# Loading w2 in one transfer of 14 rows per partition instead of one of 12 rows and eight small ones

## Chip, cores, metric

One core of a Trainium2 chip. The metric is the device time of one execution in microseconds (us); lower is better.

## The reference, cut to what matters

```python
# x: (2, 1, 512) bf16; K, V caches: (2, 32, 8192, 128) bf16; w1: (512, 1792); w2: (1792, 512)
xn  = layernorm(x)
out = x + attention(xn, k_cache, v_cache, wq) @ wo + relu(xn @ w1) @ w2
```

One decode step. The caches are 268 MB of the 280 MB that are read; w2 is 1.8 MB.

## The kernel before

The SP engine issues every large load on one queue, in the order in which the data are wanted. The dense branch (`w1`, `w2`) is computed ahead of the loop over 32 cache blocks ("steps").

```python
FA = FT - 2            # 12 rows of w2 on every partition
FB = 2 * (FT - FA)     # 4 more on 64 partitions
FJ = FA + FB
...
# SP
sp.dma_start(vs[1], wq)                                                  # 4 MB
sp.dma_start(w1_sb, B_w1...).then_inc(dW1, 16)                           # 1.8 MB
sp.dma_start(w2_sb[:, 0:FA, :], B_w2[0:P * FA, :]...).then_inc(dW2, 16)  # 1.5 MB
w2_v = B_w2[P * FA:, :].rearrange("(p j) n -> p j n", j=FB)
for p in (0, 1, 2, 3, 32, 33, 34, 35):                                   # 8 x 32 KB
    sl = slice(p, p + 29, 4)
    sp.dma_start(w2_sb[sl, FA:FA + FB, :], w2_v[sl]).then_inc(dW2b, 16)
load_k(0); load_k(1); load_v(0)                                          # 4 MB each
for t in range(NP - 2):
    sp.wait_ge(pT[NG - 1], t + 1)   # PE has transposed K of step t: its buffer is free
    load_k(t + R)
    sp.wait_ge(sW, t + 1)
    load_v(t + 1)
...                                  # last V in two halves, then wo in five pieces, then the output
# PE, ahead of the loop
for j in range(FJ):                  # h^T = (xn @ w1)^T, four matmuls for each j
    ...
for j in range(FJ):                  # y = relu(h) @ w2
    half = slice(0, HP if j >= FA else P)
    pe.matmul(y, lhsT=hT[half, j, :], rhs=w2_sb[half, j, :], ...)
```

Of the kernel before, what the change touches and what calls it, by code (L numbers as in the profile page):

```python
# [7 lines left out]
ALU = mybir.AluOpType  # L8
# [11 lines left out]
def kernel(  # L20
# [13 lines left out]
    P = 128  # L34
    HP = P // 2
# [8 lines left out]
    FT = Dff // P  # L44
# [9 lines left out]
    QH = 512 // Dh  # L54
    Z = (QG - 1) * Bsz

    FA = FT - 2
    FB = 2 * (FT - FA)
    FJ = FA + FB
    inv_sqrt = float(Dh) ** -0.5  # L60
    eps = 1e-5

# [8 lines left out]
    def sem(name):  # L71
        return tc.alloc_semaphore(name)
# [6 lines left out]
    w1_sb = w_sb[:, 0:KT * Dff].rearrange("p (kt f) -> p kt f", kt=KT)  # L79
    w2_sb = w_sb[:, KT * Dff:KT * Dff + FJ * D].rearrange("p (j n) -> p j n", j=FJ)  # L80
# [30 lines left out]
    hT = sb([P, FJ, Bsz], bf16, "hT")  # L111
# [16 lines left out]


    dX, dO, dW1 = sem("dX"), sem("dO"), sem("dW1")  # L130
    dW2, dW2b = sem("dW2"), sem("dW2b")
    dK = [sem(f"dK{i}") for i in range(R)]
    dV = [sem(f"dV{i}") for i in range(R)]
    dH = [sem(f"dH{i}") for i in range(2)]
# [7 lines left out]
    sH, sF, sZ = sem("sH"), sem("sF"), sem("sZ")  # L142
# [13 lines left out]
    )  # L156
    hp = ot[1][:, 0:FJ * Bsz].rearrange("p (j b) -> p j b", b=Bsz)
    y = Sc[1][0:Bsz, :]
# [13 lines left out]
    @(lambda f: f(nc.sync))  # L172
    def _(sp):
        sp.dma_start(w1_sb, B_w1.rearrange("(p kt) f -> p kt f", kt=KT)).then_inc(dW1, 16)
        sp.dma_start(
            w2_sb[:, 0:FA, :], B_w2[0:P * FA, :].rearrange("(p j) n -> p j n", j=FA)
        ).then_inc(dW2, 16)

        w2_v = B_w2[P * FA:, :].rearrange("(p j) n -> p j n", j=FB)
        for p in (0, 1, 2, 3, 32, 33, 34, 35):  # L180
            sl = slice(p, p + 29, 4)
            sp.dma_start(w2_sb[sl, FA:FA + FB, :], w2_v[sl]).then_inc(dW2b, 16)
        load_k(0)
        load_k(1)
        load_v(0)
        for t in range(NP - 2):
            sp.wait_ge(pT[NG - 1], t + 1)
# [3 lines that stand above are left out]
        sp.wait_ge(sW, NP - 1)  # L191
        for i in range(2):
            sl = slice(i * SLOT // 2, (i + 1) * SLOT // 2)
            sp.dma_start(  # L194
                vs[(NP - 1) % R][:, sl], V_all[(NP - 1) * P:NP * P, sl]
            ).then_inc(dH[i], 16)
        for c in range(NC):
            sl = slice(cuts[c], cuts[c + 1])
            sp.dma_start(wo_sb[:, sl, :], wo_v[:, sl, :]).then_inc(dW[c], 16)  # L199
        sp.wait_ge(sE, 1)  # L200
        sp.dma_start(
            out.rearrange("b s (c p) -> (b s c) p", p=P), osb[:]
        ).then_inc(dO, 16)
# [38 lines left out]
    def _(pe):  # L242
# [7 lines left out]
        for g in range(QG):  # L250
            for kt in range(KT):
                i = pe.matmul(  # L252
                    qp,
                    lhsT=xz[:, kt, Z - g * Bsz:Z - g * Bsz + QG * Bsz],
                    rhs=vs[1][:, (kt * QG + g) * 512:(kt * QG + g + 1) * 512],
# [3 lines left out]
        i.then_inc(sQ, 1)  # L259
        pe.wait_ge(dW1, 16)  # L260

        w1_a = w1_sb[:, :, 0:P * FA].rearrange("p kt (f j) -> p kt j f", j=FA)
        w1_b = w1_sb[:, :, P * FA:].rearrange("p kt (f j) -> p kt j f", j=FB)
        for j in range(FJ):
            for kt in range(KT):
                i = pe.matmul(  # L266
                    hp[0:HP if j >= FA else P, j, :],
                    lhsT=w1_b[:, kt, j - FA, :] if j >= FA else w1_a[:, kt, j, :],
                    rhs=xz[:, kt, Z:Z + Bsz],
                    start=(kt == 0),  # L270
                    stop=(kt == KT - 1),
                )
# [6 lines left out]
        i.then_inc(sQ, 1)  # L279
        pe.wait_ge(sF, 2)  # L280
        pe.wait_ge(dW2, 16)
        pe.wait_ge(dW2b, 16 * 8)
        for j in range(FJ):
            half = slice(0, HP if j >= FA else P)
            i = pe.matmul(  # L285
                y,
                lhsT=hT[half, j, :],
                rhs=w2_sb[half, j, :],
                start=(j == 0),
                stop=(j == FJ - 1),  # L290
            )
# [82 lines left out]
        for u in range(2):  # L374
            t = pe.matmul(dbp[:, :, u], lhsT=onesh[:, u, :], rhs=RS[:], start=True, stop=True)
        t.then_inc(sH, 1)
        for k in range(KT):
            pe.matmul(
                fin[:, k, :],
                lhsT=ys[:, k * P:(k + 1) * P],  # L380
                rhs=ident2[:],
# [10 lines left out]
        for b in range(Bsz):  # L392
            t = pe.transpose(tO[:, b, :], OTn[:, b, :], identb[:])
# [3 lines left out]
        for dq in range(DQ):  # L397
            t = pe.matmul(
                ox,
                lhsT=sel[:, dq, :],  # L400
                rhs=Ob[:, :, dq * WJ:(dq + 1) * WJ],
                start=(dq == 0),
                stop=(dq == DQ - 1),
            )
# [3 lines left out]
        for c in range(NC):  # L408
            pe.wait_ge(dW[c], 16)
            for j in range(cuts[c], cuts[c + 1]):  # L410
                for k in range(KT):
                    t = pe.matmul(
                        fin[:, k, :],
                        lhsT=wo_sb[:, j, k * P:(k + 1) * P],
                        rhs=OX[:, j, :],
# [14 lines left out]
    @(lambda f: f(nc.vector))  # L430
    def _(v):
        v.memset(eps_t[:], eps).then_inc(sV, 1)
        v.memset(onesb[:], 1.0)
        v.memset(xz[:], 0.0).then_inc(sZ, 1)
        v.memset(prm[R - 1][:], 0.0).then_inc(sP, 1)
        v.wait_ge(dX, 16)
        v.bn_stats(out=stats[:], in_=xsb[:]).then_inc(sV, 1)
        v.wait_ge(sV, 2)
        v.bn_aggr(out=mv[:], in_=stats[:]).then_inc(sV, 1)
        v.wait_ge(sA, 1)  # L440
        v.reciprocal(out=rinv[:], in_=rstd[:]).then_inc(sV, 1)
        v.wait_ge(sV, 4)

        v.tensor_scalar(
            out=xn[:],
            in0=xsb[:].rearrange("b (p kt) -> b kt p", kt=KT),
            scalar1=mv[:, 0:1],
            scalar2=rinv[:, 0:1],
            op0=ALU.subtract,
            op1=ALU.mult,  # L450
        ).then_inc(sV, 1)
        v.wait_ge(sQ, 1)
        v.wait_ge(sZ, 1)
        v.tensor_copy(xz[:, :, Z:Z + Bsz], tpx).then_inc(sV, 1)
        v.wait_ge(sQ, 2)

        v.tensor_scalar(  # L457
            out=qs[:], in0=qp, scalar1=inv_sqrt, scalar2=None, op0=ALU.mult
        ).then_inc(sV, 1)
        v.wait_ge(sF, 1)  # L460
        for sl in (slice(0, P), slice(0, FA)), (slice(0, HP), slice(FA, FJ)):
            t = v.tensor_scalar(
                out=hT[sl], in0=hp[sl], scalar1=0.0, scalar2=None, op0=ALU.max,
            )
        t.then_inc(sF, 1)
        v.wait_ge(sQ, 3)

        v.tensor_copy(
            qb[:].rearrange("p (b g l) -> p l g b", b=Bsz, l=QH),
            tpq.rearrange("p l (g b) -> p l g b", b=Bsz),  # L470
        ).then_inc(sV, 93)
        v.wait_ge(sF, 3)
        v.tensor_tensor(out=ys[:], in0=y, in1=xsb[:], op=ALU.add).then_inc(sF, 1)

        def pair(i, n):
            for e in range(NG):
                if e not in ON_ACT:
                    v.wait_ge(pT[e], n)
                    kcopy(v, e)
            v.wait_ge(sS, n)  # L480
            for u in range(2):
                half = slice(u * HP, (u + 1) * HP)
                m = v.tensor_reduce(  # L483
                    out=mcol[i][half, :], in_=S_of(i)[half, :, u], axis=AX.X, op=ALU.max
                )
            m.then_inc(sM, 1)
            v.wait_ge(sT, n)
            v.tensor_reduce(  # L488
                out=mx[i][:], in_=tr_of(i).rearrange("o (u m) -> o u m", u=2),
                axis=AX.X, op=ALU.max, negate=True,  # L490
            ).then_inc(sX, 1)

        reg = nc.alloc_register(mybir.EngineType.DVE, "pairno_v")
        v.reg_mov(reg, 0)
        with v.Fori(0, NP // R):
            for r in range(R):
                v.reg_add(reg, reg, 1)
                pair(r, reg)

        v.wait_ge(sH, 1)  # L500
        v.reciprocal(out=RD[:], in_=Sc[0][:, 0:N]).then_inc(sV, 1)
        v.wait_ge(sV, 101)
        v.wait_ge(sO, NP + 1)
        on = OTn[:].rearrange("p b h -> p (b h)")
        v.tensor_tensor(
            out=on[:, 0:N - 2], in0=OTf[:, 2:N], in1=RD[:, 0:N - 2], op=ALU.mult
        ).then_inc(sV, 1)
        v.wait_ge(sW, NP + 1)
        v.tensor_tensor(
            out=on[:, N - 2:N], in0=ot[1][:, 0:2], in1=RD[:, N - 2:N], op=ALU.mult  # L510
        ).then_inc(sV, 1)
        v.wait_ge(sH, 2)
        v.tensor_copy(Ob[:], tp[0][0:H, 0:Bsz, :]).then_inc(sV, 1)
        v.wait_ge(sH, 3)
        v.tensor_copy(
            OX[:], Sc[1][:, 0:Bsz * WJ].rearrange("p (b j) -> p j b", b=Bsz)
        ).then_inc(sV, 1)
        v.wait_ge(sH, 4)
        v.tensor_copy(yT[:], ot[0][:, 0:KT * Bsz].rearrange("p (b c) -> p b c", c=KT)).then_inc(sV, 1)
        v.wait_ge(sH, 5)  # L520
        v.tensor_copy(osb[:], tp[1][0:Bsz * KT, 0, :]).then_inc(sE, 1)
# [70 lines left out]
```

## Time and profile before

| | before |
|---|---|
| time, median | 661.26 us (3 runs, 661.19 to 661.27) |
| span of the profiled execution | 659.3 us |
| DMA busy on average / moved | over 99% / 426 GB/s |
| PE, DVE, ACT busy | 85%, 38%, 39% |

The span is the stretch that the profile covers; the time is some 2 us longer. "DMA busy" is a mean over the core's 16 DMA engines, and a transfer counts as landed when the last of them has incremented its semaphore. The prediction below shows the lines.

### The profile page before, as it was taken

The page shows a single profiled execution, that of the slowest core. Times are in us where ns is not written, and L with a number is a line of the kernel's source. Part 1 is how long each engine was busy: PE and PEld are TensorE (multiplying, and loading weights), DVE is VectorE, ACT ScalarE, POOL GpSimd, SP SyncE. Part 2 cuts the span into 40 slices and gives each one's busy share as a digit, 9 for nine tenths or more (in the row PEclk, how much of TensorE's full clock was granted, in tenths as well). Part 3 has the DMA queues.
Part 4 walks back from the last instruction along what each step waited for, and adds up shares of the span by engine and source line. Part 5 has one row for each costly group of instructions (what it writes and reads, how often), then busy time and mean ns, then how long its engine had stood idle before and what let it go on. Part 6 is the DMA issues. An engine that isn't in the chain of part 4 may idle for free.

```text
span 659.3 us, 26888 instructions
## 1 busy us (share of the span) xinstructions
PE 562.9 (85%) x12747; PEld 538.3 (82%) x12747; DVE 253.4 (38%) x437; ACT 255.9 (39%) x403; POOL 9.0 (1%) x46
## 2 busy tenths in 40 slices
PE   2998899988799787889888788979787998788796
PEld 0488898988799787888888788978787988788795
DVE  1054344433344343334434334434333444334341
ACT  1043444444334433344343434434243444334340
POOL 1000000000000000000000000000000000000000
PEclk9798899989989898999889899979899989889998
DMA  8999999999999999999999999999999999999996
GB/s 363 447 417 437 419 437 429 431 439 423 439 423 435 431 429 439 423 439 423 435 435 427 441 419 439 427 431 437 425 441 419 439 427 431 437 425 441 421 426 266
DMA packets 10670, 280.66 MB, mean 426 GB/s; under 512 B 1250, under 2 KB 1252, under 8 KB 1828
## 3 DMA queue, kind: packets, MB, share of 16 engines
q1 hardware_dynamic: 10656, 280.50, 99.1%
q8 instruction: 9, 0.15, 0.1%
q14 instruction: 1, 0.01, 0.0%
q10 hardware_dynamic: 4, 0.00, 0.0%
HBM read 280.50 MB, written 0.00 MB: 425 GB/s over the span
## 4 chain that ended last, share of the span: by engine, by line
DMA 56%; PE 39%; ACT 2%; issue 1%; SPq 0%; DVE 0%; ACTq 0%
DMA ks<-in_A_k_cache_dram 50%; PE tp L300 21%; PE Sc L307 11%; DMA w_sb<-in_A_wo_dram 4%; PE ot L320 4%; DMA vs<-in_A_wq_dram 2%; ACT kT L427 2%; PE ot L252 1%; PE Sc L285 1%; PE ot L266 1%; ACT L427 1%; SPq L199 0%; PE Sc L355 0%; PE Sc L358 0%; SPq L194 0%
## 5 line engine op out<-in xcount | busy, mean ns | idle before, releaser
L300 PE MATMUL tp<-identb,ks 128*128 128x128 bf16 x4096 | 326.0, 229 | 68.2 <-DMA ks<-in_A_k_cache_dram 67.4
L427 DVE COPY kT<-tp 128x1024 bf16<-128x1024 bf16 x320 | 219.8, 691 | 325.1 <-PE tp L300 324.9
L300 PEld LDWEIGHTS tp<-identb,ks 128*128 128x128 bf16 x4096 | 257.2, 103 | 72.1 <-DMA ks<-in_A_k_cache_dram 70.5
L427 ACT COPY kT<-tp 128x1024 bf16<-128x1024 bf16 x192 | 194.3, 1012 | 233.4 <-PE tp L300 233.4
L307 PE MATMUL Sc<-q,kT 128*128 128x64 bf16 x4096 | 216.6, 196 | 4.6 <-ACT kT L427 4.6
L307 PEld LDWEIGHTS Sc<-q,kT 128*128 128x128 bf16 x4096 | 178.8, 100 | 7.9 <-ACT kT L427 7.8
L320 PE MATMUL ot<-prm,vs 128*128 128x64 bf16 x4224 | 156.1, 192 | 4.7 <-issue 4.7
L320 PEld LDWEIGHTS ot<-prm,vs 128*128 128x128 bf16 x4224 | 139.0, 97 | 7.5 <-issue 4.9
L542 ACT COPY nm<-Sc 128x2 f32<-128x2 f32 x32 | 5.1, 160 | 118.4 <-PE Sc L358 118.4
L546 ACT ACTIVATE prm<-Sc,nm 64x128 bf16<-64x128 f32 x64 | 25.6, 401 | 4.3
L483 DVE TENSOR_REDUCE mcol<-Sc 64x1 bf16<-64x128 f32 x64 | 18.6, 291 | 17.6 <-PE Sc L307 17.2
L427 ACT ACT_TABLE_LOAD x16 | 20.5, 1283 | 2.2
L252 PE MATMUL ot<-vs,xz 128*16 128x512 bf16 x32 | 9.3, 462 | 8.8 <-DMA vs<-in_A_wq_dram 8.8
L534 ACT COPY OTf<-ot 128x2 f32 x32 | 5.1, 160 | 27.3 <-PE ot L320 27.3
L488 DVE TENSOR_REDUCE mx<-Sc 1x2 bf16<-1x128 bf16 x32 | 8.9, 279 | 16.9 <-PE Sc L355 16.9
L252 PEld LDWEIGHTS ot<-vs,xz 128*16 128x16 bf16 x32 | 3.3, 103 | 14.4 <-issue 12.0
L237 POOL COPY q<-qb 128x2 bf16<-128x2 bf16 x32 | 5.9, 187 | 590.8 <-PE Sc L307 567.5
L546 ACT ACTIVATION_READ_ACCUMULATOR prm<-Sc,nm x64 | 11.8, 185 | 0.0
L457 DVE TENSOR_SCALAR qs<-ot 16x512 bf16<-16x512 f32 x1 | 0.7, 678 | 17.9 <-PE ot L252 17.9
L355 PE MATMUL Sc<-identb,mcol 128*1 128x128 bf16 x32 | 7.0, 217 | 0.0
L285 PE MATMUL Sc<-w_sb,hT 128*2 128x512 bf16 (+1 forms) x16 | 6.0, 544 | 0.1
L358 PE MATMUL Sc<-mx,onesb 1*128 1x2 bf16 x32 | 5.5, 172 | 0.0
(56 smaller groups left out, 38.6 us busy)
## 6 DMA issues: line engine op xcount, KB each, us to landing
ks<-in_A_k_cache_dram SPq DMA_DIRECT2D x32, 4096.0 KB, 26.7
vs<-in_A_v_cache_dram SPq DMA_DIRECT2D x31, 4096.0 KB, 31.3
vs<-in_A_wq_dram SPq DMA_DIRECT2D x1, 4096.0 KB, 12.3
vs<-in_A_v_cache_dram SPq DMA_DIRECT2D x2, 2048.0 KB, 20.0
w_sb<-in_B_w_dram SPq DMA_DIRECT2D x1, 1792.0 KB, 16.1
w_sb<-in_A_wo_dram SPq DMA_DIRECT2D x1, 1792.0 KB, 26.0
w_sb<-in_B_w_dram SPq DMA_DIRECT2D x1, 1536.0 KB, 19.3
w_sb<-in_A_wo_dram SPq DMA_DIRECT2D x1, 896.0 KB, 27.7
```

The lines of the kernel that those rows point to most:

```text
L237: g.tensor_copy(q2[t % R][:], qb[:, 2 * t:2 * t + 2]).then_inc(sQ1, 1)
L252: i = pe.matmul(qp, lhsT=xz[:, kt, Z - g * Bsz:Z - g * Bsz + QG * Bsz], rhs=vs[1][:, (kt * QG + g) * 512:(kt * QG + g + 1) * 512], start=( ...
L266: i = pe.matmul(hp[0:HP if j >= FA else P, j, :], lhsT=w1_b[:, kt, j - FA, :] if j >= FA else w1_a[:, kt, j, :], rhs=xz[:, kt, Z:Z + Bsz], ...
L285: i = pe.matmul(y, lhsT=hT[half, j, :], rhs=w2_sb[half, j, :], start=(j == 0), stop=(j == FJ - 1),)
L300: t = pe.transpose(tp[e % 4][:, i, :], ks[r][:, kk * Dh:(kk + 1) * Dh], identb[:])
L307: t = pe.matmul(Sc[r][:, 2 * kk:2 * kk + 2 * REP], lhsT=kT[e % 4][:, i, :], rhs=rep(q2[r][:]), start=True, stop=True,)
L320: t = pe.matmul(ot[r][:, 0:2 * REP], lhsT=vs[r][:, kk * Dh:(kk + 1) * Dh], rhs=rep(prm[r][:, kk, :]), start=(kk == 0), stop=(kk == KB - 1),)
L355: pe.transpose(tr_of(r), mcol[r][:], identb[:]).then_inc(sT, 1)
L427: fn(kT[e % 4][:], tp[e % 4][:]).then_inc(kR[e], 1)
L483: m = v.tensor_reduce(out=mcol[i][half, :], in_=S_of(i)[half, :, u], axis=AX.X, op=ALU.max)
L488: v.tensor_reduce(out=mx[i][:], in_=tr_of(i).rearrange("o (u m) -> o u m", u=2), axis=AX.X, op=ALU.max, negate=True,).then_inc(sX, 1)
L546: x = a.activation(out=prm[i][half, :, u], in_=S_of(i)[half, :, u], func=ACTF.Exp, bias=nm[i][half, u:u + 1], scale=1.0, accum_out=RS[half ...
```

## The change

The intent is plain: w2 has 1792 = 14 x 128 rows, so one transfer with 14 rows per partition loads it, and the special half-depth matmuls, a semaphore and a second relu go. The diff, cut to its core:

```diff
-    FA = FT - 2
-    FB = 2 * (FT - FA)
-    FJ = FA + FB
+    FJ = FT
@@ SP
-        sp.dma_start(
-            w2_sb[:, 0:FA, :], B_w2[0:P * FA, :].rearrange("(p j) n -> p j n", j=FA)
-        ).then_inc(dW2, 16)
-        w2_v = B_w2[P * FA:, :].rearrange("(p j) n -> p j n", j=FB)
-        for p in (0, 1, 2, 3, 32, 33, 34, 35):
-            sl = slice(p, p + 29, 4)
-            sp.dma_start(w2_sb[sl, FA:FA + FB, :], w2_v[sl]).then_inc(dW2b, 16)
+        sp.dma_start(w2_sb, B_w2.rearrange("(p j) n -> p j n", j=FJ)).then_inc(dW2, 16)
@@ PE: first product 64 -> 56 matmuls, second 16 (4 of half depth) -> 14
-        pe.wait_ge(dW2b, 16 * 8)
-                lhsT=hT[half, j, :],
-                rhs=w2_sb[half, j, :],
+                lhsT=hT[:, j, :],
+                rhs=w2_sb[:, j, :],
@@ DVE: relu in one instruction instead of two
```

More of the change, by code (lines that the diff above doesn't have):

```diff
@@ L130 @@
     dX, dO, dW1 = sem("dX"), sem("dO"), sem("dW1")
-    dW2, dW2b = sem("dW2"), sem("dW2b")
+    dW2 = sem("dW2")
     dK = [sem(f"dK{i}") for i in range(R)]
@@ L260, in _ @@
         pe.wait_ge(dW1, 16)
-        w1_a = w1_sb[:, :, 0:P * FA].rearrange("p kt (f j) -> p kt j f", j=FA)
-        w1_b = w1_sb[:, :, P * FA:].rearrange("p kt (f j) -> p kt j f", j=FB)
+        w1_v = w1_sb[:].rearrange("p kt (f j) -> p kt j f", j=FJ)
         for j in range(FJ):
@@ L266, in _ @@
                 i = pe.matmul(
-                    hp[0:HP if j >= FA else P, j, :],
-                    lhsT=w1_b[:, kt, j - FA, :] if j >= FA else w1_a[:, kt, j, :],
+                    hp[:, j, :],
+                    lhsT=w1_v[:, kt, j, :],
                     rhs=xz[:, kt, Z:Z + Bsz],
@@ L281, in _ @@
         pe.wait_ge(dW2, 16)
-        pe.wait_ge(dW2b, 16 * 8)
         for j in range(FJ):
-            half = slice(0, HP if j >= FA else P)
             i = pe.matmul(
                 y,
-                lhsT=hT[half, j, :],
-                rhs=w2_sb[half, j, :],
+                lhsT=hT[:, j, :],
+                rhs=w2_sb[:, j, :],
                 start=(j == 0),
@@ L460, in _ @@
         v.wait_ge(sF, 1)
-        for sl in (slice(0, P), slice(0, FA)), (slice(0, HP), slice(FA, FJ)):
-            t = v.tensor_scalar(
-                out=hT[sl], in0=hp[sl], scalar1=0.0, scalar2=None, op0=ALU.max,
-            )
-        t.then_inc(sF, 1)
+        v.tensor_scalar(
+            out=hT[:], in0=hp, scalar1=0.0, scalar2=None, op0=ALU.max,
+        ).then_inc(sF, 1)
         v.wait_ge(sQ, 3)
```

## The prediction

Names in it and in the expectations: "engines 0 to 7" are the eight of the 16 DMA engines that carried the small transfers (64 packets of 4096 bytes, eight on each of eight engines, in the trace of the kernel before), "engines 8 to 15" the eight that carried none; from e8 on, "engines 0 to 3" are the four that carry the extra rows. The packet records have no engine numbers, so these are names and no more. An "instruction packet" or "fetch" is a packet of 16384 bytes on the queue that the profile calls instruction (q8, nine packets, 1.02 to 1.10 us each).

> **What bounds the kernel now.** I read the summary first, then the chain of work that ended last, the waits, the opening and closing stretch of the timeline, and last the records of single DMA packets and of single semaphore increments that the trace holds.
>
> The summary shows the DMA engines at 9 tenths or more in every slice but the first and the last, at about 430 GB/s, while PE is busy 85% and both copying engines under 40%. One queue carries it all.
>
> ```profile
> PE 562.9 (85%) x12747; PEld 538.3 (82%) x12747; DVE 253.4 (38%) x437; ACT 255.9 (39%) x403; POOL 9.0 (1%) x46
> ...
> DMA  8999999999999999999999999999999999999996
> ...
> DMA packets 10670, 280.66 MB, mean 426 GB/s; under 512 B 1250, under 2 KB 1252, under 8 KB 1828
> ...
> q1 hardware_dynamic: 10656, 280.50, 99.1%
> ...
> DMA 56%; PE 39%; ACT 2%; issue 1%; SPq 0%; DVE 0%; ACTq 0%
> ```
>
> The 39% of PE in the chain mean no PE bound: the chain steps over to PE wherever a K load was issued by PE freeing a buffer. Two lines of the waits tell the direction: the transposes sit idle for the K load in 26 of the 32 steps, and K loads are issued long before they are needed.
>
> ```profile
> PEld tp L300 <- DMA ks<-in_A_k_cache_dram: 70.5, 26, 3.5
> ...
> SPq L163 <- PE tp L300: 426.9, 30, 34.9
> ```
>
> The end of the chain says what sets the last microsecond: the last piece of wo lands, eight matmuls follow, and the small output tail.
>
> ```profile
> 625.89 29.65 DMA w_sb<-in_A_wo_dram
> 655.58 0.39 PE ot L412 x8
> 655.99 0.18 DVE yT L519
> 656.21 0.28 PE tp L421
> 656.52 0.21 DVE osb L521
> ```
>
> So the time is: when the slowest of the 16 DMA engines has moved its share of 280 MB, plus some 5.7 us of tail (655.54 landing, 661.26 median). The packet records make this sharper. A 32 KB packet advances its engine by 1209 ns (27.1 GB/s; times 16 gives 434 GB/s), alike on every engine, and I could follow all 16 engines from 22 to 66 us without a gap over some nanoseconds. Engines in such a stream never wait for one another: **an engine that falls behind at the start is still as far behind at the end.** The increments of the load semaphores, one per engine, show it:
>
> ```
> load (16 increments, one per engine)   first    last     spread us
> wq                                     12.62    13.27    0.65
> w1                                     16.91    17.54    0.63
> w2, the 12 rows                        20.60    21.23    0.63
> K of step 0                            30.42    32.20    1.78
> K of step 2                            59.56    62.58    3.02
> K of step 4                            98.52   101.61    3.08
> K of step 30                          603.59   606.76    3.16
> last piece of wo                      652.68   655.54    2.86
> ```
>
> At the last row two engines land at 655.34 and 655.54, twelve between 653.6 and 654.3, two before 652.9. The question is what put two engines 1.2 us behind the crowd, and whether the change touches it.
>
> [...]
> 1. [...] the semaphore of the eight small transfers is touched eight times while they are being issued (3.54 to 8.26 us) and 64 times (8 by 8) between 20.79 and 22.92 us. They run on eight engines only.
> 2. [...] Trace: eight chains of eight 4096-byte packets, the other eight engines none.
> [...]
> 4. [...] a 4 KB packet with its completion record advances its engine by 161 ns, against 151 ns for 4 KB inside a long packet[...]. The overhead of eight is 0.08 us per engine.
>
> **The change part by part.**
>
> *Issuing.* The issue of the 12 rows (0.43 us) becomes that of the 14, and the eight small ones leave:
>
> ```profile
> 1.44 0.40 SPq L174 DMA_DIRECT2D w_sb<-in_B_w_dram  x1
> ...
> 1.88 0.43 SPq L175 DMA_DIRECT2D w_sb<-in_B_w_dram  x1
> ...
> 2.36 5.48 SPq L182 DMA_DIRECT2D w_sb<-in_B_w_dram  x8
> ...
> 7.88 0.92 SPq L163 DMA_DIRECT2D ks<-in_A_k_cache_dram  x2
> ...
> 13.40 9.32 PE L252 MATMUL ot<-vs,xz 128*16 128x512 bf16 x32 [8.77 <-DMA vs<-in_A_wq_dram]
> ...
> 22.66 4.06 PE L266 MATMUL ot<-xz,w_sb 128*128 128x2 bf16 x64
> ...
> 27.06 5.96 PE L285 MATMUL Sc<-w_sb,hT 128*2 128x512 bf16 x16
> ...
> 32.95 1.51 PE L300 MATMUL tp<-identb,ks 128*128 128x128 bf16 x24
> ```
>
> K of step 0 is issued 5.5 us earlier, at 2.4 instead of 7.9. But its first packet starts at 20.3 us, behind wq, w1 and w2 on the same engines. Worth 0.
>
> *PE.* The first product goes from 64 to 56 matmuls: 4.06 us / 64 = 63 ns each, 0.5 us less. The second goes from 12 full and 4 half-depth to 14 full matmuls. The weight loads of the full ones come 0.43 us apart, so 14 take 6.0 us against 5.96: 0. Two DVE instructions (0.18 and 0.15 us, side by side with others, 0.25 together) become one: 0.05. PE reaches the first transpose at 32.4 instead of 32.95, if K has landed. Nothing of it counts at the end: step 2 waits for DMA again.
>
> *DMA.* Bytes stay 280.50 MB on this queue; the shares of the engines change. Before, engines 0 to 7 carry 8 packets of 12 KB and 8 of 4 KB, engines 8 to 15 only the 12 KB ones. In advance per engine, from the packet durations (460 ns and 535 ns with some 4 ns overlap, 161 ns for a small one with its completion):
> - engines 0 to 7: 8 x 456 + 8 x 161 = 4.94 us before, 8 x 531 = 4.25 after: **0.69 us less**;
> - engines 8 to 15: 8 x 456 = 3.65 before, 4.25 after: **0.60 us more**.
>
> The old form put engines 0 to 7 1.29 us behind the others, which the spread of K in step 0 shows (0.63 to 1.78). Whether levelling it helps depends on which half holds the two laggards. Between 28.9 and 75.1 us there are seven more packets, of 16384 bytes, on the instruction queue; each pushes the engine it falls on back by about 1.2 us. Following the engines packet by packet from the small transfers on, those at 28.93, 41.2 and 48.41 fall on engines 8 to 15, those at 55.68 and 61.92 on engines 0 to 7. The landings place the last two: of the early group five are left at 59.6, four at 69.4 and three at 79.1, so both fell on engines 8 to 15. Lateness against an unhit engine of 8 to 15 is therefore 0 (three engines), about 1.2 (five hit ones of 8 to 15 and six unhit ones of 0 to 7) and 2.5 (two hit ones of 0 to 7): exactly the pattern of the last landing, so the laggards are engines of the half that the change relieves.
>
> After, with the same hits: unhit engines at 0.60, hit ones of 8 to 15 at 1.2 + 0.6 = 1.8, hit ones of 0 to 7 at 2.5 - 0.69 = 1.8. The latest moves from 2.5 to 1.8. By absolute times: 655.54 - 0.69 = 654.85, and the latest of the middle, 654.26 + 0.60 = 654.86. Both give a last landing at 654.85, **0.65 to 0.7 us earlier**. The tail behind it is unchanged, and PE, which without waits for wo would be done at about 654.4, moves along. Sum: 661.26 - 0.66 = **660.6 us**.
>
> **The rivals.**
> - *Nothing, to 0.1 us.* The removed work was hidden anyway: right for issuing and PE. For it: total bytes and rate are fixed. Against it: the end follows the slowest engine, not the mean. It would give 661.2.
> - *Slower by 0.6 us.* If the laggards were engines 8 to 15 hit twice, the change would load them further: 661.9. The landing pattern alone cannot tell this from my reading (both give 3, 11 and 2 engines), only the packet-by-packet tracking does; I trust it to 66 us, where it had no mismatch.
> - *The instruction packets move.* PE has ten matmuls, some 20 instructions, fewer ahead of the loop, so the points of these fetches shift. If they choose other engines, one hit twice is late by 0.6 + 2 x 1.2 = 3.0: 0.5 us later than now, 661.8. Two more such packets come at 650.19 and 653.71; if one hit an already late engine it would cost up to 1.2. The one at 650.19 now hits an early one (three early engines at 649.4, two at 651.3). If the hits spread better, nothing beats about 1.8 as long as one engine is hit at all, so this rival only adds. I give it one in five.
> - *A large win from fewer transfers.* The 5.5 us of issuing lie ahead of K packets that wait until 20.3 us anyway: no view supports it.
>
> **Range and chances.** Two thirds of the weight lie at 660.4 to 660.9, a fifth at 661.2 to 661.9[...]. Range 659.9 to 661.8. A 2% change is 13.2 us; no mechanism above reaches a tenth of it. Faster 0.01, same 0.98, slower 0.01.
>
> **What would show it.** Right: 64 packets of 4 KB and 64 completions gone (10542 packets, 1186 under 512 B); K of step 0 issued near 2.4 us yet landing no earlier than 31.5; its landings in one group plus one hit engine, not in two groups; last wo landing near 654.85 with about seven engines in the late group and no pair behind it; the distance from the last landing to the end unchanged. Wrong: a last landing at or after 655.5, or a late pair still there (then the hits moved or the halves were told apart wrongly); the transposes no longer waiting for K; a tail longer than 5.7 us.

## More of the kernel before

All runs quoted are of state "fast". The effects here are far under 1%, so profiles and single landings carry the argument and the times only confirm it.

One more view is needed later: the two dense products ahead of the loop, as busy time per engine with the TensorE clock that the throttle granted (PEclk).

```profile
22.66:26.72 4.06, 4.06 (x67) 4.03 (x67) 0.68 (x1) 0.00 (x0) 0.00 (x0) 0.77 1.10 476
27.06:33.02 5.96, 5.96 (x18) 1.66 (x19) 0.41 (x1) 0.00 (x0) 0.31 (x2) 0.61 1.02 437
```

Columns: stretch, its length, busy time (and instructions) of PE, PEld, DVE, ACT, POOL, PEclk, DMA share, GB/s. Both products ran at a reduced granted clock, 0.77 and 0.61.

## The result

| | before | after |
|---|---|---|
| time, median of 5 | 661.27 us (661.19 to 661.34) | 660.85 us (660.73 to 662.65) |
| profiled span | 659.3 us | 658.7 us |
| last piece of wo landed | 655.54 us | 654.86 us |

The ratio is the mean time of the one kernel's fast runs over that of the other's in the same rounds, so not quite the ratio of the medians: 0.9998, 95% interval 0.9986 to 1.001. One execution of 662.65 us among five pulls it up; the other four are 660.73 to 660.88. By the 2% rule: same. Two later calls timed the changed kernel again: 660.89 against 661.39, and 660.78 against 661.35. The three differences of medians are 0.42, 0.50 and 0.57 us.

The page of the changed kernel, the lines that answer to those in the prediction:

```profile
PE 559.9 (85%) x12737; PEld 536.7 (81%) x12737; DVE 253.2 (38%) x436; ACT 255.8 (39%) x403; POOL 8.8 (1%) x46
...
DMA  8999999999999999999999999999999999999996
...
DMA packets 10542, 280.66 MB, mean 426 GB/s; under 512 B 1186, under 2 KB 1188, under 8 KB 1700
...
q1 hardware_dynamic: 10528, 280.50, 99.1%
...
DMA 58%; PE 37%; ACT 2%; issue 1%; SPq 1%; ACTq 0%; DVE 0%
```

Ten matmuls and 128 packets are gone (64 data packets, 64 completions); DMA is as full as before. The waits, who waited for whom (us, times, longest):

```profile
PEld tp L288 <- DMA ks<-in_A_k_cache_dram: 71.5, 27, 3.5
...
SPq L161 <- PE tp L288: 430.5, 30, 41.0
```

PE still waits for K, in 27 steps instead of 26: the added one is step 0. The timeline of the opening (start, length, engine):

```profile
1.43 0.42 SPq L172 DMA_DIRECT2D w_sb<-in_B_w_dram  x1
...
1.89 0.42 SPq L173 DMA_DIRECT2D w_sb<-in_B_w_dram  x1
...
2.36 1.01 SPq L161 DMA_DIRECT2D ks<-in_A_k_cache_dram  x2
...
21.77 3.52 PE L256 MATMUL ot<-xz,w_sb 128*128 128x2 bf16 x56
...
25.57 4.87 PE L273 MATMUL Sc<-w_sb,hT 128*2 128x512 bf16 x14
...
32.82 2.22 PE L288 MATMUL tp<-identb,ks 128*128 128x128 bf16 x24 [2.38 <-DMA ks<-in_A_k_cache_dram]
```

K is issued at 2.36 us instead of 7.88 and PE is done with its products at 30.44 instead of 33.02. Yet the first transpose starts at 32.82 instead of 32.95: the wait for K (2.38 us) has eaten the rest. And the end of the chain:

```profile
626.04 28.81 DMA w_sb<-in_A_wo_dram
...
654.90 0.39 PE ot L400 x8
...
655.32 0.18 DVE yT L505
...
655.54 0.28 PE tp L409
...
655.85 0.21 DVE osb L507
```

Everything from the last landing on is the same as before, 0.67 to 0.68 us earlier. The landings by engine show why. In an ordinary fence, the 16 increments of the semaphore of K of step 0 and of the last piece of wo, sorted:

```
K of step 0
before 30.42 30.56 30.67 30.68 30.69 30.82 30.94 | 31.60 31.66 31.86 31.90 31.92 32.03 32.07 32.09 32.20
after  30.89 31.13 31.15 31.15 31.15 31.18 31.25 31.30 31.31 31.32 31.33 31.35 31.38 31.39 31.41 | 32.77
last piece of wo
before 652.68 652.89 | 653.61 653.86 653.89 653.92 654.00 654.04 654.10 654.22 654.23 654.24 654.26 654.26 | 655.34 655.54
after  652.84 653.05 653.14 653.15 653.23 653.26 653.30 653.32 | 654.53 654.59 654.60 654.75 654.79 654.81 654.82 654.86
```

Two groups became one plus one engine hit by a fetch (at 27.18 us), and at the end three levels became two.

### The profile page after: what moved, and what is told of

Same layout as the page of the kernel before. It is cut to its first block, busy times and chain, and to the rows that moved or that the text cites. A ratio compares the mean times of both kernels' runs of the same rounds, so it can differ in the third digit from the quotient of the medians.

```text
span 658.7 us, 26859 instructions
## 1 busy us (share of the span) xinstructions
PE 559.9 (85%) x12737; PEld 536.7 (81%) x12737; DVE 253.2 (38%) x436; ACT 255.8 (39%) x403; POOL 8.8 (1%) x46
## 4 chain that ended last, share of the span: by engine, by line
DMA 58%; PE 37%; ACT 2%; issue 1%; SPq 1%; ACTq 0%; DVE 0%
DMA ks<-in_A_k_cache_dram 54%; PE tp L288 21%; PE Sc L295 11%; PE ot L308 4%; DMA w_sb<-in_A_wo_dram 4%; ACT kT L415 2%; ACT L415 1%; SPq L190 0%; PE Sc L343 0%; SPq L185 0%; PE Sc L346 0%; SPq L173 0%; SPq L172 0%; SPq L166 0%; PE ot L400 0%
## 5 line engine op out<-in xcount | busy, mean ns | idle before, releaser
L308 PEld LDWEIGHTS ot<-prm,vs 128*128 128x128 bf16 x4224 | 140.5, 98 | 6.2 <-issue 3.6
L469 DVE TENSOR_REDUCE mcol<-Sc 64x1 bf16<-64x128 f32 x64 | 18.6, 291 | 20.0 <-PE Sc L295 19.5
L400 PE MATMUL ot<-OX,w_sb 128*128 128x2 bf16 x128 | 4.0, 166 | 1.1 <-DMA w_sb<-in_A_wo_dram 0.7
## 6 DMA issues: line engine op xcount, KB each, us to landing
vs<-in_A_v_cache_dram SPq DMA_DIRECT2D x31, 4096.0 KB, 31.3
```

What stands on the lines that cost most here:

```text
L308: t = pe.matmul(ot[r][:, 0:2 * REP], lhsT=vs[r][:, kk * Dh:(kk + 1) * Dh], rhs=rep(prm[r][:, kk, :]), start=(kk == 0), stop=(kk == KB - 1),)
L469: m = v.tensor_reduce(out=mcol[i][half, :], in_=S_of(i)[half, :, u], axis=AX.X, op=ALU.max)
```

## The experiments

Theory: the time is set by the slowest DMA engine; the small transfers loaded engines 0 to 7 alone, and lateness gained at the start stays to the end. Rivals: the number of transfers or SP's time to issue them; PE's shorter prologue and its moved fetches; nothing but chance. Every kernel below computed the right result. Each ran five times beside nine runs of the kernel before in its call; the medians of before were 661.31, 661.39 and 661.35 in the three calls.

| run | median us (range) | profiled execution: last wo landing |
|---|---|---|
| e1 rows 10 + 8 | 661.93 (661.69 to 661.99) | 655.91 |
| e2 even, eight of 16 partitions | 661.69 (661.60 to 661.78) | 655.76 |
| e3 small ones from ACT | 661.52 (661.25 to 661.78) | 655.39 |
| e4 K issued late | 660.83 (660.75 to 661.41) | 654.90 |
| e5 changed kernel again | 660.89 (660.77 to 662.29) | 655.23 |
| e6 rows 13 + 2 | 661.32 (661.19 to 661.41) | 655.52 |
| e7 PE extra | 660.97 (660.84 to 661.07) | 654.99 |
| e8 four engines | 661.60 (661.37 to 661.64) | 655.75 |
| e9 seven full transfers | 661.32 (661.27 to 661.38) | 655.55 |
| e10 four engines, aligned | 660.79 (660.52 to 661.07) | 655.03 |
| e11 four engines, crossed | 661.79 (661.42 to 662.31) | 655.53 |
| e12 changed kernel, third | 660.78 (660.73 to 661.05) | 654.91 |

### e1: more of the imbalance

```diff
-    FA = FT - 2
+    FA = FT - 4
```

> 10 rows on all 128 partitions and 8 rows on 64 (still eight small transfers), so the number of transfers and of bytes stays that of the kernel before and only the share of engines 0 to 7 grows. Engine-balance theory: these engines take 8 x 0.380 + 8 x 0.312 = 5.54 us for w2 instead of 4.94, the others 3.04 instead of 3.65; a late pair in every load, last landing 655.54 + 0.60 = 656.1, time 0.4 to 0.6 us over the kernel before, about 661.8. Rival that the number of transfers or their issue matters: as before, 661.27. Rival that nothing matters: as before too.

661.93, which is 0.62 above before: with the number and issue of transfers unchanged, only the share of engines 0 to 7 cost time. (PE has ten matmuls more as well; e7 shows that ten count for nothing.) The gap that the small transfers open is seen best where K of step 0 lands: seven engines at 29.92 to 30.36, a hit one at 31.83, eight at 32.37 to 32.72, so 2.4 us between the groups; 5.54 - 3.04 = 2.5 was expected. The last landing, 655.91, is 0.2 short of the expected 656.1: followed packet by packet, the two engines of 0 to 7 that an instruction fetch hit were 0.2 us ahead of the last of their group at K of step 0.

### e2: even shares, small transfers kept

```diff
# to the changed kernel
-        sp.dma_start(w2_sb, w2_v).then_inc(dW2, 16)
+        sp.dma_start(w2_sb[:, 0:FJ - 2, :], w2_v[:, 0:FJ - 2, :]).then_inc(dW2, 16)
+        for p in range(0, P, 16):
+            sl = slice(p, p + 16)
+            sp.dma_start(w2_sb[sl, FJ - 2:FJ, :], w2_v[sl, FJ - 2:FJ, :]).then_inc(dW2b, 16)
```

> 12 rows on all partitions in one transfer and the other 2 rows by eight small transfers of 16 partitions each, one partition per engine: all engines carry the same, as in the changed kernel, but there are nine transfers and the long issue as in the kernel before. Engine-balance theory: as the changed kernel plus 8 times 10 ns, last landing about 654.95, time 660.8 to 660.95. Rival that fewer transfers or earlier K issue brought the gain: as before, 661.27.

A miss: 661.69, worse than before. The shares are as meant: against the changed kernel the page has 256 packets more (10798), 128 of them under 512 B (1314), so 128 small packets and as many completions, sixteen of each per transfer. The landings are as even as in the changed kernel (K of step 0: fifteen engines at 31.58 to 32.22, a hit one at 33.49), but all are some 0.6 us later. So not uneven shares, but something in these small transfers slowed every engine. Each transfer here takes 16 neighbouring partitions, and not every fourth as in the kernel before; e9 to e11 look into the number of transfers and the order of their partitions.

### e3: the issue moved off SP

```diff
# to the kernel before: the eight issues leave SP, and ACT has them after its sqrt
-            sp.dma_start(w2_sb[sl, FA:FA + FB, :], w2_v[sl]).then_inc(dW2b, 16)
+            a.dma_start(w2_sb[sl, FA:FA + FB, :], w2_v[sl]).then_inc(dW2b, 16)
```

> The kernel before with its eight small transfers issued from ACT, so that K is issued about 5.5 us earlier (near 2.4 us) while engines 0 to 7 keep their extra 32 KB. Engine-balance theory: last landing within 0.15 us of 655.54, time 661.2 to 661.35. Rival that the issue time of SP mattered: as the changed kernel, 660.85.

```profile
2.36 1.06 SPq L163 DMA_DIRECT2D ks<-in_A_k_cache_dram  x2
```

In the timeline of this run K is issued at 2.36, as in the changed kernel, and nothing is gained: 661.52, last landing 655.39, a late pair again (655.36 and 655.39, the next at 654.37). The landing is as expected; the time is 0.17 over the expected range, which stays open. The edit did more than move the issue: the small packets ran from 7.6 to 18.3 us, among those of wq and w1, and not after the 12 rows. The gap at K of step 0 is there all the same (seven engines at 30.49 to 30.86, the others from 31.83 on).

### e4: K issued later than ever

```diff
# to the changed kernel
+        sp.wait_ge(dV[1], 16)
         load_k(0)
         load_k(1)
```

> The changed kernel with the first K and V loads issued only when wq has landed, at about 13.2 us, later than in the kernel before (7.9). Queued work on the engines reaches to 21.7 us. Engine-balance theory: no change from the changed kernel, 660.8 to 660.9, last landing near 654.86. Rival of the issue time: at or above the kernel before, 661.3 or more.

```profile
13.18 0.80 SPq L161 DMA_DIRECT2D ks<-in_A_k_cache_dram  x2
```

Issued at 13.18 us and as fast as the changed kernel: 660.83, last landing 654.90. With e3 this refutes the rival of SP's issue time from both sides.

### e5 and e12: the changed kernel again

No edit.

> The changed kernel once more, on another chip or another day, beside the others of this call: a reference for them, and a look at how often an execution like the 662.65 us one comes. Engine-balance theory: median 660.75 to 660.95, last landing 654.8 to 654.95, seven late engines. If 660.85 was luck: as the kernel before, 661.3.

> The changed kernel as a reference on the chip of this call, and five more executions for the count of those that come out over 662. Median 660.8 to 660.95; if the slow ones come one in five, one here.

Medians 660.89 and 660.78, on two different chips: the gain comes again. A slow execution came once in the five of e5 (662.29) and not in e12; over the three sets it is two of fifteen (662.65 and 662.29), while none of the 32 executions of the kernel before went over 661.73. No profile fell on one, so their cause stays open. The profile of e5 (an execution of 661.07) has its last landing at 655.23, outside the expected 654.8 to 654.95, which those of the changed kernel (654.86) and of e12 (654.91) meet: single executions of one kernel differ by 0.3 us or more.

### e6: half of the imbalance

```diff
-    FA = FT - 2
+    FA = FT - 1
```

> 13 rows on all partitions and 2 rows on 64 by the same eight small transfers: half of the extra share that engines 0 to 7 have in the kernel before. For w2 they take 8 x 0.494 + 8 x 0.085 = 4.63 us, between 4.25 (changed kernel) and 4.94 (before). Engine-balance theory: last landing 654.86 + 0.38 = 655.24, time about 661.1, between the two. Rival that the number of transfers or their issue decides: as before, 661.3.

At K of step 0 the groups are as expected: the early one at 30.70 to 31.20, the late at 31.42 to 32.02, medians 0.7 us apart (4.63 - 3.95 = 0.68 expected). The time, 661.32, is 0.2 over the expected 661.1, and about that of the kernel before (661.35). Together with the changed kernel (0), before (1.29 expected, 1.25 measured between medians) and e1 (2.5 and 2.4), the gap at the start follows the sum well; the end follows in order only, changed, then 13 + 2 and 12 + 4 alike, then 10 + 8.

The packet records show what the expectation left out. While the small transfers ran, five of the 32 KB packets took 1.31 to 1.38 us instead of 1.21, although the small transfers took every fourth partition as in the kernel before. Followed packet by packet, the two engines of this half that a fetch hit later (at 54.39 and 60.63 us) had each lost 0.2 us in this way, most of the 0.28 us by which the last landing (655.52) missed the expected 655.24. Why these packets of 2 KB slow the K packets, when those of 4 KB in the kernel before and of 8 KB in e1 and e10 do not, stays open.

### e7: PE's work put back

```diff
# to the changed kernel: ten useless transposes of the same tile first
-        for l in range(QH):
+        for l in (0,) * 10 + tuple(range(QH)):
```

> The changed kernel with ten more (useless) small transposes on PE ahead of the loop, so that PE has as many matmuls there as in the kernel before and its instruction fetches lie where they were, while the transfers stay even. Engine-balance theory: as the changed kernel, within 0.15 us, last landing near 654.86. Rival that the ten matmuls saved on PE or the moved fetches brought the gain: as the kernel before, 661.3.

PE has its 12747 matmuls back, the seventh instruction fetch is back at 75.8 us (it had moved from 75.1 to 108.3 in the changed kernel; the first stays where the changed kernel has it, at 27.1), and the time is 660.97, last landing 654.99. The rival of the saved matmuls falls.

### e8: the extra rows on four engines

```diff
-    FA = FT - 2
-    FB = 2 * (FT - FA)
+    FA = FT - 1
+    FB = 4 * (FT - FA)          # 4 rows on 32 partitions
-        for p in (0, 1, 2, 3, 32, 33, 34, 35):
-            sl = slice(p, p + 29, 4)
+        for p in range(8):
+            sl = slice(p, p + 25, 8)
```

> 13 rows on all 128 partitions and the other 128 rows, 4 each, on 32 partitions by eight small transfers of four partitions, thus on engines 0 to 3 alone. For w2 these four take 8 x 0.494 + 8 x 0.161 = 5.24 us against 4.25 in the changed kernel, the other twelve 3.95. Engine-balance theory: with no instruction fetch on engines 0 to 3 the latest are then the fetch-hit ones of the others, 0.3 us earlier than in the changed kernel (last landing 654.55, time 660.55); with one on them they are 1.0 us later (last landing 655.85, time 661.8). Rival that nothing matters: 660.85 to 661.3.

Neither branch. The pattern is that of "no fetch on engines 0 to 3": from K of step 0 (four engines at 32.86 to 32.98) to the landing near 110 us (four at 110.56 to 110.68) these keep their distance, while seven of the other twelve are pushed back, to 111.05 to 111.36. But all engines land about 0.7 us later than worked out, and the time is 661.60. This is e2 again: K packets of 32 KB that take 1.21 us elsewhere took up to 2.05 us while the small transfers ran, and 4 KB packets up to 0.34 us instead of 0.16.

### e9: seven full transfers

```diff
# to the changed kernel
-        sp.dma_start(w2_sb, w2_v).then_inc(dW2, 16)
+        for j in range(0, FJ, 2):
+            sp.dma_start(w2_sb[:, j:j + 2, :], w2_v[:, j:j + 2, :]).then_inc(dW2, 16)
```

> w2 in seven transfers of two rows on all 128 partitions: even over the engines as in the changed kernel[...], but in 56 packets of 2 KB with seven completions per engine. From the measured 84 ns of such a packet (80 ns of advance) w2 takes 56 x 0.080 + 7 x 0.005 = 4.52 us per engine against 4.25. Engine-balance theory[...]: last landing 654.86 + 0.27 = 655.1, time 661.1. If instead many small transfers cost as much as in that run (its crowd landed K of step 0 some 0.6 us later than in the changed kernel): last landing 655.6 or later, time 661.6.

661.32, between the two expectations. The landings of the seven transfers come 0.66 to 0.69 us apart, 4.72 us in all (from 17.66 to 22.38 for the latest increment), where the one transfer of 14 rows takes 4.29 (17.40 to 21.69). I had summed 4.52. The added 0.43 us equals what the time rose over e5, 661.32 - 660.89 = 0.43. So cutting up a transfer does cost time, some 0.06 us a piece here, on every engine and through to the end. No packet of 2 KB took longer than 0.098 us, so this is not the trouble of e2 and e8.

### e10 and e11: aligned and crossed

e10 is e8 with 8 rows on 16 partitions in four transfers, each of every fourth partition of the 16 ("aligned"). e11 changes one line of e10 and takes four neighbours each ("crossed"); both words stand here only for these two orders:

```diff
         for p in range(4):
-            sl = slice(p, p + 13, 4)          # e10: partitions p, p+4, p+8, p+12
+            sl = slice(4 * p, 4 * p + 4)      # e11: four neighbours
```

> As the four-engine run, but [...] 8 rows each, in four transfers. That run showed no instruction fetch on engines 0 to 3, and an unexpected 0.7 us on all engines while the small transfers ran. [...] engines 0 to 3 take 5.2 us for w2 (0.95 more than in the changed kernel, to about 654.3 at the end), the fetch-hit others 0.3 less, last landing 654.56, time 660.55, the fastest so far. If any small transfer on few engines delays all: last landing near 655.3, time 661.2 or more.

The first of e10's two branches is that the delay of e8 is gone with this order.

> The same as the aligned four-engine run in bytes, sizes and number, with one thing changed: each of the four transfers takes four neighbouring partitions[...]. If crossing is what cost 0.7 us: first K packets of other engines take well over 1.21 us, K of step 0 lands 0.5 us or more later than in the aligned run, time 0.5 us or more above it. If the cause was the number of small packets or something else: equal to the aligned run.

The 32 KB packets that started between 19.5 and 24.5 us, from the packet records:

```
run                 longest us   over 1.3 us
before                 1.213          0
changed                1.213          0
e10 aligned            1.213          0
e11 crossed            1.818         16
e2 (16 neighbours)     1.768         19
e8 (every eighth)      2.045         25
e6 (every fourth)      1.382          5
e9 (all 128)           1.252          0
```

One line, the same bytes and packets: the order of the partitions costs 661.79 - 660.79 = 1.0 us in the medians. K of step 0 lands on its last engine at 33.48 us instead of 32.56; the crowd of unloaded engines hardly moves (30.76 to 31.38 against 30.68 to 31.40), unlike in e2 and e8. The chain's end in e10 and e11:

```profile
625.36 29.68 DMA w_sb<-in_A_wo_dram
```

```profile
626.97 28.56 DMA w_sb<-in_A_wo_dram
```

Start and length add up to 655.04 and 655.53: 0.5 us apart in these two executions (661.02 and 661.51). The line also changes which rows of w2 are read side by side, so whether reading or writing makes the difference is not shown. Nor does every fourth partition always avoid it: e6 has that order and five packets over 1.3 us. Why the order counts is not shown. Why engines that the small transfers did not use were slowed as well is not shown.

As the fastest version e10 missed: 660.79 against 660.78 for e12, and not 660.55. The four loaded engines came out where they should (K of step 0 at 31.97 to 32.40; 31.3 of the changed kernel's crowd plus 0.95 was expected), but the latest two were others: two engines that were already 0.4 us behind the crowd at K of step 0 (31.37 and 31.40), and already at wq (13.40 and 13.41, the next at 13.16). Followed packet by packet, they are the ones that the fetches at 41.86 and 74.64 hit. The 0.3 us won was lost to start scatter: the 16 engines do not start together (in the profile of the changed kernel their first 32 KB packets start from 1.99 to 3.02 us), and 0.52 us of that is left when wq lands there (12.59 to 13.11). No version here beats the changed kernel.

## Why the prediction was right

**The number and its mechanism.** 660.6 was predicted, 660.85 measured, within the range of 659.9 to 661.8. The last landing was predicted at 654.85 and profiled at 654.86. That it hits so closely is partly luck: other executions of the same kernel gave 654.91 and 655.23. The gain in time is 0.42 to 0.57 us where 0.66 was predicted. The profiled execution supports 0.68 up to the last landing; the span then ends 3.80 us later, as before, and from there to the reported time it is 2.13 us instead of 1.92. So the tail outside the span was 0.21 longer than I took it. Over the 27 runs of the kernel before that remainder is 1.96 to 2.21 us (spans are listed to 0.1), so I had built on a reference at the short end of it. The mis-sized term is "some 5.7 us of tail": it was 5.93 in the profiled execution of the changed kernel. In the two calls that list the spans of both kernels, their medians differ by 0.6 and 0.5 us, about the predicted amount.

**Issuing: worth 0.** Right; e3 and e4 show it in both directions.

**PE: nothing counts at the end.** Right (e7), but not for the reason given. "Step 2 waits for DMA again" is a misreading: after step 0 the transposes next wait for K at 140.5 us in the kernel before and at 139.8 in the changed one. The 26 waits all lie from there to the end; e7 shows only that PE's saving is worth nothing there. A size was off too: the second product took 4.87 us, not 6.0. I took the spacing of 0.43 us between its matmuls as fixed. It was a matter of the granted clock:

```profile
21.77:25.22 3.45, 3.45 (x57) 3.44 (x57) 0.68 (x1) 0.00 (x0) 0.00 (x0) 1.00 1.05 456
25.57:30.44 4.87, 4.87 (x14) 1.43 (x14) 0.44 (x1) 0.00 (x0) 0.30 (x2) 0.65 1.02 434
```

The same view as before: 1.00 and 0.65 instead of 0.77 and 0.61. Within the second product the matmuls came 0.43 us apart from 26.61 to 30.02 us, at a granted clock of 0.50, and 0.22 us apart ahead of that, at 1.00. PE was ready at 30.44 and stood until 32.82: what it saved became a wait.

**DMA: 0.69 us less on engines 0 to 7, 0.60 more on the others.** Right at its source. The gap at K of step 0 follows the sums over four doses (0, 0.7, 1.25, 2.4 measured for 0, 0.68, 1.29, 2.5), and in the kernel before it is carried to the end: the late pair of the last landing is 1.08 us behind the next engine (655.34 against 654.26).

**The laggards are engines 0 to 7.** Borne out: had they been engines of the other half, the change would have cost 0.6 us. e1, which loads engines 0 to 7 more, is slower. Followed once more to 80 us in the trace of the kernel before, with the number of packets per load as a check, the fetches at 55.68 and 61.92 fall on engines 0 to 7 and the other five on 8 to 15, as the prediction has it. Only the push was mis-sized: on an engine's own landings, two successive loads are 9.71 us apart, and 11.25 with a fetch between, so a fetch costs 1.5 us and not 1.2. It stands on both sides of the comparison and cancels.

**The rival of moved fetches.** They did move, the first from 28.93 to 27.18 and the seventh from 75.1 to 108.3, and still hit seven engines once each. The late group at the end has eight engines, not "about seven": the fetch at 649.56 pushed one more back, an early one. Putting PE's instructions back (e7) moved the seventh fetch back and changed nothing.

**What I understated.** "The overhead of eight is 0.08 us per engine" holds for the kernel before, whose small transfers stretched no K packet (longest 1.213 us). It does not hold in general: e2, e8 and e11 are 0.7 to 1.0 us slower than the changed kernel or e10 (e2 against e4), with 16 to 128 small packets. Had I taken it for a rule, I would have got e2 wrong, and did.

## What to carry to other kernels

In this stream, with the DMA engines over 99% busy, lateness stayed: in the kernel before the spread of a load's 16 increments was 3.02 us at 62.6 us and 3.16 at 606.8. So the end was set by the engine with the largest sum of bytes, late start and interruptions: look at the 16 increments of one load's semaphore, early and late in the run, not at the mean bandwidth, which was 426 GB/s before and after. A transfer on fewer engines shifts that sum (by 1.25 us here, at K of step 0), and a small one is worth its place only if it levels it. Where small transfers are needed, try more than one order of their partitions (661.79 us crossed against 660.79 aligned), and look for stretched packets all the same. Work saved on an engine that waits for DMA turned into waiting: PE was done with its products 2.58 us earlier (30.44 instead of 33.02) and then waited 2.38 us for K.
